# Second chunk of batch 0 in pairs of head pairs, and earlier exps in batches 2 and 3

## The chip, the cores and the metric

The kernel runs on one core of a Trainium2 chip. A core has five engines with instruction streams of their own: TensorE (matmul; weight loads are shown apart, as PEld), VectorE (DVE), ScalarE (ACT), GpSimd (POOL) and SyncE (SP), which here issues DMAs only. The metric is device time in microseconds for one whole execution. Before the change it is 401.13 us, the median of 3 runs (400.8 to 401.75).

## The reference, cut to what matters

Eight batches, eight heads, 1024 positions, head size 64. Keys and values are first projected along the sequence to 64 rows, then comes ordinary attention, then a feed-forward layer that takes the largest of three products.

```python
k_proj = np.einsum('ks,bhsd->bhkd', E, k)
v_proj = np.einsum('ks,bhsd->bhkd', F, v)
scores = scale * np.matmul(q, k_proj.transpose(0, 1, 3, 2))
attn = softmax(scores)
a = np.matmul(attn, v_proj)            # then heads are joined to x: 8192 x 512
h = np.maximum(np.maximum(x @ w1, x @ w2), x @ w3)   # 512 -> 768
out = h @ w_out                        # 768 -> 512
```

## The kernel before, in words

A batch is 1024 tokens, worked on in two chunks of 512 (`ch` 0 and 1). The attention works on head pairs: `g` counts the 4 pairs, `hp` the two heads in a pair. The feed-forward layer of a batch runs step by step, and the attention of the next batch is put between its steps.

**A chunk of the feed-forward layer.** `up` has six steps (`jt` 0 to 5), each with 12 matmuls of 128x512 (3 weight matrices by 4 blocks `ct`, line 600). ScalarE copies the first product out (`h1s`, line 665), VectorE takes the two maxima (lines 669 and 610; the last writes `hT`). Then `down` has four steps of 6 matmuls (line 708), each copied out to `o_sb` (by VectorE in batch 0, by ScalarE later) and stored by SP. The very first chunk of all has another order, `up_first`: it sweeps over w1, then over w2, then over w3, holding one bank for each of the six `jt`; a sweep does the first two `ct` for all `jt` ("a"), then the last two, with a max per `jt`.

**The order is written out.** `plan(b)` gives, by chunk and step, the functions that are issued behind that step. Steps 0 to 5 are those of `up`, 6 to 9 are `down`. [...] `then` in `up_first` does the same for the first chunk, with keys such as (2, 4): sweep 2 (w3), `jt` 4. Work put in `later` is issued at the next `run_later`, which comes behind the `h1s` copy of an `up` step or the o_sb copy of a `down` step.

**Banks.** Everything that TensorE writes goes to the eight banks of PSUM. `bank()` and `two()` (an even pair) choose the bank, or the pair, that is free first by the planner's own running clock (`clock`, `free`); this happens while the program is built. On the chip the choice only decides what a matmul has to wait for: the last reader of that bank.

**Attention of one head pair.** `scores` (line 221): four matmuls on quarters of the array (64*64) into two banks. `exps` (line 232): ScalarE's exp, to `pT`. Then either `za`, which has `sums` (ones times `pT`), `values` (`vp` times `pT`, both line 241), `invert` (ScalarE: ln to `zl`, line 301, and exp of its negative to `zi`, line 307) and `scale_x` (VectorE: product to `xT`, line 318); or, from batch 2 on, `zc`, which forms the sums of all four head pairs in one bank by eight matmuls (line 266), inverts them at once and spreads them through DRAM (`zd`, `zi_all`), with `vx` for values and scale. `sc(..., now=True)` issues the exp at once; without it, the exp goes to `later`.

**Batch 0.** Only its first chunk's attention is done before the feed-forward layer starts. The attention of its second chunk (`c1`: positions 4 to 7) is done one head pair at a time, between the w3 sweep and `down` of the first chunk; all its instructions have half the columns (256 per matmul, 512 per exp). It must be in `xT` before `up(0, 1, 0)`, whose first three matmuls per weight matrix read head pairs 0, 1 and 2; pair 3 is read at the end of the step.

**q of later batches.** `qd(b)` packs q by four VectorE copies to `q_p` (line 102) and has SP issue a DMA transpose to `qT` (line 421), for batch 1 in two halves. The next load of q, by POOL's queue, waits for the last of them.

Of the kernel before, what the change touches and what calls it, by code (L numbers as in the profile page):

```python
# [15 lines left out]
def kernel(  # L16
# [13 lines left out]
    nc = tc.nc  # L30
# [46 lines left out]
    def two():  # L77
        n = min(range(0, 8, 2), key=lambda n: max(free[n:n + 2]))
        deal((n, n + 1))
        return psum_t[:, n:n + 2, :], (n, n + 1)  # L80
# [6 lines left out]
    def pe(dt, wait=0.0):  # L87
        clock["pe"] = max(clock["pe"], wait) + dt
        return clock["pe"]

    def runs(eng, ready, dt, ns=()):
        if eng in clock:
            clock[eng] = max(clock[eng], ready + 0.06) + dt
            for n in ns:
                free[n] = clock[eng]
            return clock[eng]
        return ready + dt
# [3 lines left out]
    def copy(eng, o, i, ns=(), dt=0.65):  # L101
        done = {  # L102
            "v": nc.vector.tensor_copy, "s": nc.scalar.copy, "g": nc.gpsimd.tensor_copy
        }[eng](out=o, in_=i)
        runs(eng, clock["pe"] if ns else 0.0, dt, ns)
        return done
# [100 lines left out]
    def k_pair(b, g):  # L207
        if b in turned:
            return kpTs[b][:, g % 2, (g // 2) * KP:(g // 2 + 1) * KP]
        return kpTs[b][:, g, :]  # L210
# [3 lines left out]
    def scores(b, g, lo, nsi):  # L214
        t, ns = two()
        n = nsi // 2
        for c in range(2):
            for hp in range(2):
                rows = slice(hp * HALF, (hp + 1) * HALF)
                at = g * SI + lo + c * n  # L220
                nc.tensor.matmul(  # L221
                    out=t[c * HALF:(c + 1) * HALF, hp, 0:n * P],
                    lhsT=k_pair(b, g)[rows],
                    rhs=qTs[b][rows, at:at + n, :],
                    start=True, stop=True,
                )
        return t[:, :, 0:n * P], ns, pe(n * MM / 4 + 0.1)
# [20 lines left out]
    def sums(b, g, lo, nsi):  # L248
        return pair_mm(b, g, lo, nsi, lambda rows, hp: ones[rows])
# [48 lines left out]
    def invert(b, g, lo, nsi, z):  # L298
        t, ns, ready = z
        zl = att.tile([P, 2, CHUNK], FP32, name="zl", bufs=1)[:, :, 0:nsi * HALF]  # L300
        nc.scalar.activation(out=zl, in_=t, func=AF.Ln)  # L301
        runs("s", ready, 0.17 + nsi * 0.107, ns)
        if nsi == SI:
            zi = zi_all(b)[:, g]
        else:
            zi = att.tile([P, 2, CHUNK // 2], FP32, name="zi0", bufs=4)
        nc.scalar.activation(out=zi, in_=zl, func=AF.Exp, scale=-1.0)  # L307
        zis[b, g, lo] = zi, runs("s", ready, 0.17 + nsi * 0.107)

    def values(b, g, lo, nsi):  # L310
        if b not in xTs:
            xTs[b] = att.tile([P, NCT, SI, P], BF16, name="xT")
        return pair_mm(b, g, lo, nsi, lambda rows, hp: vps[b][rows, 2 * g + hp, :])
# [17 lines left out]
    def sc(b, g, lo=0, nsi=SI, now=False):  # L331
        def f():
            t = scores(b, g, lo, nsi)
            if now:
                exps(b, g, lo, nsi, t)
            else:
                later.append(lambda: exps(b, g, lo, nsi, t))
        return f

    def za(b, g, lo=0, nsi=SI, then=False):  # L340
        def f():
            z = sums(b, g, lo, nsi)
            av = values(b, g, lo, nsi)
            invert(b, g, lo, nsi, z)
            if then:
                later.append(lambda: scale_x(b, g, lo, nsi, av))
            else:
                scale_x(b, g, lo, nsi, av)
        return f
# [56 lines left out]
            )  # L406
        return f

    def qd(b, parts=1):

        def f():
            q_p = att.tile([P, NPAIR, SI, 2, D], BF16, name="q_p", bufs=1)
            qTs[b] = att.tile([P, NPAIR * SI, P], BF16, name="qT")
            n = NPAIR // parts
            for lo in range(0, NPAIR, n):
                for g in range(lo, lo + n):
                    copy(
                        "v", q_p[:, g].rearrange("p si h d -> p h si d"),
                        qkv[b][0][:, 2 * g:2 * g + 2], (), 0.43,
                    )  # L420
                last_T[b] = nc.sync.dma_start_transpose(
                    out=qTs[b][:, lo * SI:(lo + n) * SI, :],
                    in_=q_p[:, lo:lo + n].rearrange("p g si h d -> p (g si h d)"),
                )
        return f

    kps = {}
    def kproj(b):
# [312 lines left out]
    def plan(b):  # L741
        n = b + 1
        if b == 0:
            c1 = (SPC, SPC)
            return {
                (0, 6): [za(0, 1, *c1), sc(0, 3, *c1)],
                (0, 7): [qd(1, 2), store_now, za(0, 2, *c1)],
                (0, 8): [za(0, 3, *c1)],
                (1, 1): [kproj(1)],
                (1, 2): [kt(1)],  # L750
                (1, 3): [sc(1, 0, now=True), sc(1, 1), vproj(1), ld(2)],
                (1, 4): [za(1, 0), sc(1, 2, now=True)],
                (1, 5): [za(1, 1), sc(1, 3)],
                (1, 7): [za(1, 2)],
                (1, 8): [za(1, 3)],
            }
        if b == 1:
            return {
                (0, 0): [qd(2)],
                (0, 3): [kproj(2), vproj(2), ld(3, (0,))],  # L760
                (0, 4): [kt(2)],
                (0, 5): [sc(2, 0, now=True), sc(2, 1, now=True), sc(2, 2)],
                (0, 6): [sc(2, 3)],
                (0, 8): [zc(2, nc.gpsimd), ld(3, (1, 2))],
                (1, 1): [qd(3)],
                (1, 3): [vx(2, 0), vx(2, 1)],
                (1, 6): [vx(2, 2), vx(2, 3)],
            }
        if b == 2:
            return {  # L770
                (0, 2): [kproj(3), vproj(3), ld(4)],
                (0, 3): [kt(3)],
                (0, 4): [sc(3, 0, now=True), sc(3, 1)],
                (0, 5): [sc(3, 2, now=True), sc(3, 3)],
                (0, 7): [zc(3)],
                (0, 8): [qd(4)],
                (1, 3): [kproj(4), vproj(4), ld(5), vx(3, 0), vx(3, 1)],
                (1, 4): [kt(4)],
                (1, 7): [vx(3, 2), vx(3, 3), sc(4, 0)],
            }  # L780
        if n == B:
            return {}
        out = {
            (0, 1): [sc(n, 1, now=True), sc(n, 2, now=True), sc(n, 3)],
            (0, 3): [zc(n)],
            (1, 2): [vx(n, 0), vx(n, 1)],
            (1, 6): [vx(n, 2), vx(n, 3)],
        }
        if n + 1 < B:
            out[0, 4] = [qd(n + 1)]  # L790
            out[1, 2] = [kproj(n + 1), kd(n + 1), vproj(n + 1)] + out[1, 2]
            out[1, 6] += [sc(n + 1, 0)]
        if n + 2 < B:
            out[1, 3] = [ld(n + 2)]
        return out

    for b in range(B):
        p = plan(b)

        def behind(ch, step):  # L800
            for f in p.get((ch, step), []):
                f()

        for ch in range(NCHUNK):
            if (b, ch) == (0, 0):
                c1 = (SPC, SPC)
                up_first({
                    (0, 0, 1): [lambda: x(1)],
                    (0, 0, 3): [lambda: z(2), lambda: z(3)],
                    (0, 1, 1): [lambda: v_pair(2)],  # L810
                    (0, 1, 3): [lambda: x(2)],
                    (0, 1, 5): [lambda: v_pair(3), ld(1)],
                    (0, 2, 1): [lambda: x(3)],
                    (2, "a", 0): [pack_q(0, (0, 1), *c1)],
                    (2, "a", 1): [pack_q(0, (2, 3), *c1)],
                    (2, "a", 3): [qp(0, (0, 1), *c1)],
                    (2, "a", 5): [qp(0, (2, 3), *c1)],
                    (2, 1): [sc(0, 0, *c1)],
                    (2, 2): [sc(0, 1, *c1)],
                    (2, 4): [za(0, 0, *c1, then=True), sc(0, 2, *c1)],  # L820
                })
                run_later()
                behind(0, NJT - 1)
            else:
                for step in range(NJT):
                    up(b, ch, step, lambda: behind(ch, (step, "mid")))
                    behind(ch, step)
            for tt in range(SPC):
                down(b, ch, tt, "v" if b == 0 else "s")
                behind(ch, NJT + tt)  # L830
# [30 lines left out]
```

## Time and profile before

| | |
|---|---|
| Median of 3 runs | 401.13 us |
| The profiled execution's own time | 401.58 us |
| Its span, first to last instruction | 399.8 us |
| TensorE busy | 388.2 us, 97% of the span |
| VectorE busy | 203.0 us, 51% |
| ScalarE busy | 151.4 us, 38% |
| GpSimd busy | 34.4 us, 9% |
| Granted TensorE clock | full, 1.00 |

In a line of the profile stand the engine, the line of the kernel, the operation, what is written and read, the shape and the count. In a timeline a line starts with its start and its length in us; instructions of one kind that follow each other are merged, and `x4` tells how many. A bracket at the end names the idle time of the engine just before, and what ended it. Matmul ends are modelled, so lines may overlap a little, and some matmul records can be missing: a group of six can stand there with five. SPq is the queue of SP; its rows are the issuing of DMAs, not their transfer.

### The profile page before, as it was taken

How to read it: one execution, taken by the hardware profiler on the slowest of the kernel's cores; microseconds unless marked ns; L12 is line 12 of the kernel's file. 1: busy time of each engine (PE TensorE's matmuls, PEld its weight loads, DVE VectorE, ACT ScalarE, POOL GpSimd, SP SyncE). 2: the span in 40 equal slices, each digit the busy share in tenths (PEclk: the TensorE clock that was granted, in tenths of full speed). 3: DMA queues.
4: the chain of work that ended last, by engine and by line, in shares of the span. 5: the costliest groups of instructions: out<-in, count | busy, mean ns of one | idle time of the engine just before them, and what ended most of it. 6: DMA issues, size and time to landing. Idle time of an engine off the chain costs nothing.

```text
span 399.8 us, 5713 instructions
## 1 busy us (share of the span) xinstructions
PE 388.2 (97%) x2244; PEld 176.5 (44%) x2286; DVE 203.0 (51%) x316; ACT 151.4 (38%) x243; POOL 34.4 (9%) x49
## 2 busy tenths in 40 slices
PE   6899999999999999999999999999999999999996
PEld 3544443453444445444454445444454444444443
DVE  2348756761674525736273544744266342745251
ACT  2534538527222452263323532245323533132322
POOL 7350011000400200110002000200000000000000
PEclk9999999999999999999999999999999999999999
DMA  8999999977899998999989979696980229020203
GB/s 145 206 206 207 205 242 144 240 148 155 217 186 207 209 224 185 239 174 206 217 218 132 254 161 266 106 228 132 212 216 20 89 75 244 0 105 2 105 0 107
DMA packets 67340, 66.31 MB, mean 166 GB/s; under 512 B 31505, under 2 KB 59793, under 8 KB 67313
## 3 DMA queue, kind: packets, MB, share of 16 engines
q0 software_dynamic: 29104, 30.41, 47.3%
q1 hardware_dynamic: 38064, 35.46, 34.9%
q8 instruction: 18, 0.29, 0.3%
q10 hardware_dynamic: 144, 0.07, 0.1%
q14 instruction: 10, 0.07, 0.1%
HBM read 69.73 MB, written 16.97 MB: 217 GB/s over the span
## 4 chain that ended last, share of the span: by engine, by line
PE 87%; DMA 7%; POOL 2%; ACT 2%; issue 1%; DVE 1%; ACTq 0%; POOLq 0%
PE banks L600 59%; PE banks L708 19%; DMA qT<-q_p 4%; DMA v_t<-in_v_dram 3%; PE banks L355 3%; PE banks L241 2%; PE banks L221 2%; PE banks L266 1%; ACT zl L301 1%; ACT zi_all L307 1%; POOL k_t L152 0%; POOL q_t L157 0%; POOL v_t L152 0%; PE banks L688 0%; DVE xT L318 0%
## 5 line engine op out<-in xcount | busy, mean ns | idle before, releaser
L600 PE MATMUL banks<-xT,w_sb 128*128 128x512 bf16 x1119 | 254.7, 379 | 2.5 <-issue 0.6
L600 PEld LDWEIGHTS <-w_sb 128*128 128x128 bf16 x1152 | 110.1, 98 | 136.4 <-issue 8.1
L669 DVE TENSOR_TENSOR m<-banks,h1s 128x512 f32<-128x512 f32 x90 | 62.1, 690 | 134.7 <-ACT h1s L665 90.9
L665 ACT COPY h1s<-banks 128x512 f32<-128x512 f32 x90 | 52.6, 585 | 122.2 <-PE banks L600 120.7
L708 PE MATMUL banks<-wout_sb,hT 128*128 128x512 bf16 x370 | 85.8, 379 | 0.9 <-issue 0.6
L610 DVE TENSOR_TENSOR hT<-banks,m 128x512 bf16<-128x512 f32 x90 | 62.3, 692 | 9.4
L708 PEld LDWEIGHTS <-hT 128*128 128x128 bf16 x378 | 35.3, 98 | 47.4 <-issue 5.6
L102 ACT COPY o_sb<-banks 128x512 f32<-128x512 f32 (+2 forms) x57 | 32.8, 577 | 58.2 <-PE banks L708 57.9
L232 ACT ACTIVATE pT<-banks 128x1024 bf16<-128x1024 f32 (+1 forms) x36 | 32.8, 931 | 18.5 <-PE banks L221 18.5
L318 DVE TENSOR_TENSOR xT<-banks,zi_all 128x1024 bf16<-128x1024 f32 x28 | 33.1, 1220 | 11.7 <-PE banks L241 6.9
L201 POOL DMA_DIRECT2D q_t<-in_q_dram x7 | 6.1, 878 | 197.9 <-DMA qT<-q_p 118.1
L102 DVE CAST vp<-banks 64x256 bf16<-64x256 f32 (+1 forms) x18 | 7.1, 397 | 11.9 <-ACT vp L102 9.0
L355 PEld LDWEIGHTS <-efT 128*64 128x64 bf16 x224 | 11.6, 110 | 3.4 <-issue 3.4
L102 ACT CAST vp<-banks 64x256 bf16<-64x256 f32 x14 | 5.1, 364 | 18.4 <-PE banks L355 18.3
L221 PE MATMUL banks<-qT,kpT 64*64 64x512 bf16 (+1 forms) x144 | 11.4, 362 | 0.6 <-DVE m L669 0.3
L241 PE MATMUL banks<-pT,vp 64*64 64x512 bf16 (+1 forms) x144 | 11.4, 364 | 0.3 <-DVE vp L102 0.2
L301 ACT ACTIVATE zl<-banks 128x512 f32<-128x512 f32 (+1 forms) x12 | 8.9, 739 | 5.6 <-PE banks L241 4.6
L102 DVE COPY q_p<-q_t 128x1024 bf16<-128x1024 bf16 x28 | 10.5, 436 | 0.5 <-DMA q_t<-in_q_dram 0.5
L102 DVE COPY o_sb<-banks 128x512 f32<-128x512 f32 (+1 forms) x9 | 5.7, 639 | 4.5 <-PE banks L688 4.5
L355 PE MATMUL banks<-k_t,efT 128*64 128x256 bf16 x112 | 7.4, 276 | 0.0
L355 PE MATMUL banks<-v_t,efT 128*64 128x256 bf16 x112 | 7.3, 273 | 0.0
L478 PE MATMUL banks<-warm_f 128*128 128x512 f32 x8 | 5.8, 861 | 1.5 <-DVE warm_f L175 1.5
(63 smaller groups left out, 119.0 us busy)
## 6 DMA issues: line engine op xcount, KB each, us to landing
out_dram<-o_sb SPq DMA_DIRECT2D x30, 512.0 KB, 4.5
zi_all<-zd SPq DMA_DIRECT2D x20, 512.0 KB, 7.7
q_t<-in_q_dram POOLq DMA_DIRECT2D x7, 1024.0 KB, 10.4
k_t<-in_k_dram POOLq DMA_DIRECT2D x7, 1024.0 KB, 16.6
v_t<-in_v_dram POOLq DMA_DIRECT2D x7, 1024.0 KB, 21.5
zi_all<-zd POOLq DMA_DIRECT2D x4, 512.0 KB, 7.9
w_sb<-in_moe_w_dram POOLq DMA_DIRECT2D x4, 384.0 KB, 11.2
k_t<-in_k_dram POOLq DMA_DIRECT2D x2, 512.0 KB, 9.2
```

What stands on the lines that cost most here:

```text
L102: done = {"v": nc.vector.tensor_copy, "s": nc.scalar.copy, "g": nc.gpsimd.tensor_copy}[eng](out=o, in_=i)
L221: nc.tensor.matmul(out=t[c * HALF:(c + 1) * HALF, hp, 0:n * P], lhsT=k_pair(b, g)[rows], rhs=qTs[b][rows, at:at + n, :], start=True, stop= ...
L232: nc.scalar.activation(out=pTs[b, g, lo], in_=t, func=AF.Exp, scale=scale)
L241: nc.tensor.matmul(out=t[hp * HALF:(hp + 1) * HALF, c, 0:nsi * HALF], lhsT=w(rows, hp), rhs=p[rows, hp, :], start=True, stop=True,)
L301: nc.scalar.activation(out=zl, in_=t, func=AF.Ln)
L318: nc.vector.tensor_tensor(out=xTs[b][:, g, lo:lo + nsi, :].rearrange("a (c s) p -> a c (s p)", c=2), in0=t, in1=zi, op=ALU.mult,)
L355: nc.tensor.matmul(out=t[hh * HALF:(hh + 1) * HALF, 0:width], lhsT=efT[:, si, (kv - 1) * KP:kv * KP], rhs=qkv[b][kv][:, heads[hh], si, :], ...
L600: nc.tensor.matmul(out=h, lhsT=w_sb[i][:, ct, jt * P:(jt + 1) * P], rhs=xTs[b][:, ct, ch * SPC:(ch + 1) * SPC, :], start=(ct == first), st ...
L610: nc.vector.tensor_tensor(out=o, in0=h, in1=other, op=ALU.max)
L665: nc.scalar.copy(out=h1s, in_=h[0][0])
L669: nc.vector.tensor_tensor(out=m12, in0=h[1][0], in1=h1s, op=ALU.max)
L708: nc.tensor.matmul(out=o_ps, lhsT=hTs[b, ch][:, jt, tt * P:(tt + 1) * P], rhs=wout_sb[:, jt, :], start=(jt == 0), stop=(jt == NJT - 1),)
```

## The change

**Second chunk of batch 0.** Two head pairs go side by side in each bank. The new class `Duo` holds two head pairs (`u` 0: pairs 0 and 1, `u` 1: pairs 2 and 3); its methods issue eight matmuls of 256 columns where four were issued per head pair, and one exp, ln, exp or product of 1024 columns where two of 512 were. The attention is visited behind (2, 1) with the scores of duo 0, behind (2, 4) with its sums and values and the scores of duo 1, and behind the first `down` step, (0, 6), with the sums and values of duo 1. The visits behind (2, 2), (0, 7) and (0, 8) are gone from TensorE; VectorE's and ScalarE's parts are placed by hand.

**q of batch 1.** Behind (0, 7) the first two copies to `q_p` stay on VectorE, with their transpose; the scale of duo 1 follows; the other two copies go to ScalarE, with their transpose; `store_now`, the held-back store, comes last.

**Batches 2 and 3.** The exp of the fourth head pair is issued at once instead of at the next `run_later`.

```diff
-    def qd(b, parts=1):
+    def qd(b, gs=range(NPAIR), eng="v"):
...
+    class Duo:
+        def __init__(self, u, lo):
+            self.u, self.lo, self.n = u, lo, SPC * HALF
+        def part(self, t, gi):
+            return t[:, :, gi * self.n:(gi + 1) * self.n]
+        def scores(self):
+            t, ns = two()
+            for gi in range(2):
+                for c in range(2):
+                    for hp in range(2):
+                        rows = slice(hp * HALF, (hp + 1) * HALF)
+                        at = (2 * self.u + gi) * SI + self.lo + c * SPC // 2
+                        nc.tensor.matmul(
+                            out=self.part(t, gi)[c * HALF:(c + 1) * HALF, hp],
+                            lhsT=k_pair(0, 2 * self.u + gi)[rows],
+                            rhs=qTs[0][rows, at:at + SPC // 2, :],
+                            start=True, stop=True,
+                        )
+            ready = pe(0.3)
+            self.p = att.tile([P, 2, CHUNK], BF16, name="pT", bufs=6)
+            nc.scalar.activation(out=self.p, in_=t, func=AF.Exp, scale=scale)
+            runs("s", ready, 1.03, ns)
+        def pairs(self, w):
...
+        def sums(self):
+            t, ns, ready = self.pairs(lambda rows, h: ones[rows])
+            self.zl = att.tile([P, 2, CHUNK], FP32, name="zl", bufs=1)
+            nc.scalar.activation(out=self.zl, in_=t, func=AF.Ln)
+            runs("s", ready, 1.03, ns)
+        def values(self):
+            self.av = self.pairs(lambda rows, h: vps[0][rows, h, :])
+        def invert(self):
+            self.zi = zi_all(0)[:, self.u]
+            nc.scalar.activation(out=self.zi, in_=self.zl, func=AF.Exp, scale=-1.0)
+            self.when = runs("s", clock["pe"], 1.06)
+        def scale(self):
+            t, ns, ready = self.av
+            nc.vector.tensor_tensor(
+                out=xTs[0][:, 2 * self.u:2 * self.u + 2, self.lo:self.lo + SPC, :]
+                .rearrange("a g (c s) p -> a c g (s p)", c=2),
+                in0=t.rearrange("a c (g x) -> a c g x", g=2),
+                in1=self.zi.rearrange("a c (g x) -> a c g x", g=2), op=ALU.mult,
+            )
+            runs("v", max(ready, self.when), 1.22, ns)
...
-                (0, 6): [za(0, 1, *c1), sc(0, 3, *c1)],
-                (0, 7): [qd(1, 2), store_now, za(0, 2, *c1)],
-                (0, 8): [za(0, 3, *c1)],
+                (0, 6): [
+                    duo[1].sums, duo[1].values, duo[0].scale, duo[1].invert,
+                ],
+                (0, 7): [
+                    qd(1, range(2)), duo[1].scale, qd(1, range(2, 4), "s"), store_now,
+                ],
...
-                (0, 6): [sc(2, 3)],
+                (0, 6): [sc(2, 3, now=True)],
...
-                (0, 5): [sc(3, 2, now=True), sc(3, 3)],
+                (0, 5): [sc(3, 2, now=True), sc(3, 3, now=True)],
...
-                    (2, 1): [sc(0, 0, *c1)],
-                    (2, 2): [sc(0, 1, *c1)],
-                    (2, 4): [za(0, 0, *c1, then=True), sc(0, 2, *c1)],
+                    (2, 1): [duo[0].scores],
+                    (2, 4): [
+                        duo[0].sums, duo[0].values, duo[1].scores, duo[0].invert,
+                    ],
```

## The prediction

> **What bounds the kernel now.** I read the page's busy shares and chain first, then the timeline of TensorE through the stretch that the diff rewrites, then the matmuls of `zc`, then the chain around 150 to 170 us.
>
> ```profile
> PE 388.2 (97%) x2244; PEld 176.5 (44%) x2286; DVE 203.0 (51%) x316; ACT 151.4 (38%) x243; POOL 34.4 (9%) x49
> ...
> PE 87%; DMA 7%; POOL 2%; ACT 2%; issue 1%; DVE 1%; ACTq 0%; POOLq 0%
> ```
>
> TensorE is the bound: what makes its stream shorter, or takes a wait out of it, is gained, and nothing else counts unless TensorE is made to wait. The stream around the change (start, length, count):
>
> ```profile
> 35.26 0.81 PE L600 MATMUL banks<-xT,w_sb 128*128 128x512 bf16 x3
> 36.00 0.30 PE L221 MATMUL banks<-qT,kpT 64*64 64x256 bf16 x4
> 36.24 0.60 PE L600 MATMUL banks<-xT,w_sb 128*128 128x512 bf16 x2
> 37.01 0.30 PE L221 MATMUL banks<-qT,kpT 64*64 64x256 bf16 x4 [0.16 <-ACT pT L232]
> 37.24 1.04 PE L600 MATMUL banks<-xT,w_sb 128*128 128x512 bf16 x4
> ...
> 38.87 0.61 PE L600 MATMUL banks<-xT,w_sb 128*128 128x512 bf16 x2
> 39.31 1.46 PE L708 MATMUL banks<-wout_sb,hT 128*128 128x512 bf16 x6
> ...
> 41.38 1.24 PE L708 MATMUL banks<-wout_sb,hT 128*128 128x512 bf16 x5 [0.16 <-issue]
> ...
> 43.14 1.47 PE L708 MATMUL banks<-wout_sb,hT 128*128 128x512 bf16 x6
> 44.54 0.30 PE L241 MATMUL banks<-pT,ones 64*64 64x256 bf16 x4
> 44.67 0.28 PE L241 MATMUL banks<-pT,vp 64*64 64x256 bf16 x4
> 44.89 1.47 PE L708 MATMUL banks<-wout_sb,hT 128*128 128x512 bf16 x6
> 46.19 4.05 PE L600 MATMUL banks<-xT,w_sb 128*128 128x512 bf16 x17
> ```
>
> A 512-column matmul starts every 0.216 us (46.19 less 44.89, by six). What a visit to the attention takes is the distance between two long rows, less 0.216 per long matmul. The x5 row is a group of six with one record missing, so the visit before it is shorter by 0.216:
> - visit of (2, 1): 36.24-35.26-3x0.216 = 0.33, one group of four small matmuls
> - (2, 2): 37.24-36.24-2x0.216 = 0.57, one group; the row says that it waits for an exp, 0.24 over the first
> - (2, 4): 38.87-37.24-4x0.216 = 0.77, three groups
> - (0, 6): 41.38-39.31-6x0.216-0.216 = 0.56, three groups
> - (0, 7): 43.14-41.38-5x0.216 = 0.68, two groups
> - (0, 8): 44.89-43.14-6x0.216 = 0.45, two groups.
>
> Together 3.36. An undisturbed visit is 0.33 with one group, 0.45 with two and 0.56 with three: each further group costs 0.115, so going in and out costs 0.215. Against that (2, 4) waits 0.2 and (0, 7) 0.23; with (2, 2), 0.67 us of the six visits is waiting.
>
> **First part: the three visits of the duos.** All twelve groups remain, so clean visits would be 0.45 (two groups), 0.91 (six) and 0.68 (four), 2.04. At the switch a rule of the Trainium skill is weighed. The row: 0.215 per visit, so three visits fewer save 0.65. The rule: "TensorEngine Tiling (Array Packing)", section "Key Properties", says that a change of tiling mode drains the engine, and "TensorE: Matmul & The Clock Gate", section "Step-by-step: what each phase is for", puts a drain at about 128 cycles of 2.4 GHz, 0.053 us. One at each of two switches would be an estimate of 0.11 per visit, 0.32 for three. The row is twice that and is taken; by the rule the forecast would end 0.33 later.
>
> New waits, followed with the old durations. ACT rows are 0.60 for 512 columns and 1.03 (exp, `zl`) or 1.06 (`zi_all`) for 1024; a max on VectorE is 0.68 at a pitch of 0.60, a 1024-column `xT` scale 1.22. Banks come from the planner's own clock, gone through by hand from its state at (2, 1): `duo[0].scores` takes pair 2/3, its sums 6/7, its values 2/3, `duo[1].scores` 4/5, the first down bank 6, `duo[1].sums` 4/5, values 0/1.
> - 36.00 scores of duo 0 (eight matmuls); exp 36.47 to 37.50. Long matmuls from 36.36 on, six of them; the second visit starts 37.75, after that exp: the 0.24 wait of (2, 2) is gone.
> - 37.75 sums, values, and at 38.20 scores of duo 1. Bank 5 still belongs to the fourth max of the last w3 sweep (jt 3), which ends 38.33: a wait of 0.2, as (2, 4) has now. The visit ends 38.75.
> - `zl` of duo 0 runs 38.22 to 39.25 and holds bank 6, which the first down group wants at 39.18: a new wait of 0.13. Behind it on TensorE is everything.
> - exp of duo 1 ends 40.2; third visit 40.70 to 41.30, no wait. Three down groups, and the first `up` of chunk 1 starts at 45.18 instead of 46.19.
>
> So the first part gives 3.36-(2.04+0.2+0.13) = 1.0 us.
>
> What hides the rest. VectorE: o_sb 40.80, duo 0 scale 41.45 to 42.67 (its `zi` is ready at 41.3), o_sb, two q_p copies 43.42 to 44.16, duo 1 scale to 45.35. The third matmul of that `up` reads head pair 2 at 45.6: cover 0.25, and beyond it each us costs one. The new scale has a four-dimensional output pattern that no row shows; nearest is the 1.22 us scale of the same 1024 elements. Below nothing it can't help; if each took 0.5 longer, 0.75 would be lost. I take 1.22. ScalarE does two q_p copies of 1024 elements after `zi` of duo 1 (43.4). The second rule weighed: VectorE's four copies are one row,
>
> ```profile
> 43.61 1.42 DVE L102 COPY q_p<-q_t 128x1024 bf16<-128x1024 bf16 x4
> ```
>
> so some 0.35 apiece, while ScalarE's 512-element q_p copies take 0.61. "ScalarE: Activation LUTs", section "What ACT_TABLE_LOAD costs", gives one element per cycle for every type, 0.186 us + 0.833 ns each: 1.04 a copy, which speaks against the move; twice the row would be 1.22. The second half is ready at 45.5 or 45.9. Neither costs anything: SP is held by the first half until 51.3,
>
> ```profile
> 44.39 11.74 SPq L421 DMA_TRANSPOSE qT<-q_p  x2
> ```
>
> and its next ScalarE work, `h1s`, is due at 47.5. `store_now` sits behind both transposes on SP as before, and POOL's next load still waits for the second one. The first half's landing (44.39+12.1 by the DMA view, 56.5) doesn't move with TensorE, which now asks for it at 56.9 instead of 57.9: cover 0.4, and lost one for one beyond. In chunk 1 the bank choices come out as the same pattern with other numbers, so its waits (some 0.9 us from 65 to 76, for exps, a max and a scale) stay.
>
> **Second part: exps at once.** The exp of the fourth head pair now comes in front of an o_sb copy instead of behind the next one, and `zc` needs it:
>
> ```profile
> 96.24 1.03 ACT L232 ACTIVATE pT<-banks 128x1024 bf16<-128x1024 f32 x1
> 96.94 0.97 PE L266 MATMUL banks<-pT,pick 128*32 128x512 bf16 x8
> 97.84 1.47 PE L708 MATMUL banks<-wout_sb,hT 128*128 128x512 bf16 x6
> ```
>
> From the first `zc` matmul to the next long one is 0.90 here and in batch 3 (142.82 to 143.72). A later batch, whose exps are long done, shows 0.55:
>
> ```profile
> 182.47 0.62 PE L266 MATMUL banks<-pT,pick 128*32 128x512 bf16 x8
> 183.02 1.25 PE L600 MATMUL banks<-xT,w_sb 128*128 128x512 bf16 x5
> ```
>
> The exp moves from 96.24 to 95.5 (right behind the one before it) and from 142.12 to 141.05: done before 96.9 and 142.8. Gain 2x0.35 = 0.70. The o_sb copy queued behind waits up to 0.8; its bank isn't wanted soon and its store has slack.
>
> **Where some of it is given back.** One transfer has no slack:
>
> ```profile
> 153.59 14.56 DMA qT<-q_p
> ...
> 168.19 0.41 PE banks L221 x4
> ```
>
> Batch 4's scores wait for this landing, already 0.28 us. By then TensorE is 1.7 early. The landing's chain hangs on the program's progress (qT of batch 3 issued at 107.10, behind VectorE; its landing releases batch 4's loads; these crowd `zd` from 145.11 to 150.7, which releases `zi_all` and then this transpose), so it comes earlier by the 1.35 gained before 107; whether the last 0.35 gets through the crowd is open: cost 0 to 0.35, I take 0.2.
>
> **Sum.** 1.0+0.7-0.2 = 1.5: the profiled span 399.8 becomes 398.3, the profiled execution's own 401.58 becomes 400.1; it lies 0.45 over the median shown, 401.13, which becomes 399.6. About 0.2% (0.8 us) is what a measurement of this kernel can tell from no change.
>
> **Rivals.**
> - The first part comes to almost nothing: a bank falls otherwise than by my hand count, or the wide scale is slow, and TensorE waits in the duos as it did in the six visits. For it: three covers there are under 0.4 us. Against: ScalarE and VectorE lose fixed costs (1.2 becomes 1.03 per pair). Then only 0.7 is left: 400.4.
> - Nothing is gained, for the landing at 168.15 is set by the DMA engines' load and stays put: TensorE gives all of it back there, 401.1. For it: DMA shares at 1.2 from 107 to 150. Against: around 85 to 100 that share is 0.77, so the backlog starts anew behind program progress.
> - Slower: the qT transpose of batch 4 lands later than now. `zd` needed 5.6 us there against 2.4 at 230.83, because batch 4's loads fill the queues; `zi_all` and the transpose queue behind it on SP, and a meeting with other packets could cost some us. TensorE pays one for one: from a landing at 169.0 (0.8 later than now) the kernel is slower by over 0.2%; at 169.2, 402.2. Against: all its sources move earlier together.
>
> **How the numbers follow.** Forecast 0.66, centre 399.6, own range 399.0 to 400.2; little gained in the duos 0.13; nothing gained 0.10; slower 0.11. The range leaves out under 2 in 10 if it reaches from 399.0 to the no-gain case at 401.2. Faster by over 0.8: the forecast and half of the first rival, 0.71; within 0.2%: the other half and the no-gain case, 0.17; slower 0.12.
>
> **What would show it.** Three visits between 36 and 41.5; the first `up` of chunk 1 at 45.2; a 0.2 wait for a max in the second visit and 0.13 before the first down group; `zc` at 0.55 in batches 2 and 3; scores of batch 4 near 166.6 with a wait of 0.3 to 0.6 for the transpose. It would be wrong if that `up` starts after 46, if TensorE waits for the xT scale at 45.6 or for qT at 56.9, or if batch 4's scores start at 168 or later.

## The result, and the profile after

The changed kernel takes 399.44 us (median of 6 runs, 398.88 to 399.63), the kernel before 400.97 in the same comparison (6 runs): 0.9961 of it, 95% interval 0.9947 to 0.9974. That is 1.53 us faster, and by the interval between 1.0 and 2.1; 1.5 was forecast. (Ratios, here and below, are worked out from all the runs, and needn't equal the quotient of the two medians.) The profiled execution took 399.43 us with a span of 397.7; the one of before had 401.58 and 399.8.

Line numbers have moved: the matmuls of `up` are now line 668, those of `down` line 776, the maxima lines 678 and 737, and `Duo` has lines 446 (scores), 454 (exp), 463 (sums and values), 474 and 482 (ln, inverse) and 487 (scale). The timeline of TensorE in the changed kernel, through the stretch that was rewritten:

```profile
35.72 0.41 PE L446 MATMUL banks<-qT,kpT 64*64 64x256 bf16 x8
36.06 1.47 PE L668 MATMUL banks<-xT,w_sb 128*128 128x512 bf16 x6
37.47 0.41 PE L463 MATMUL banks<-pT,ones 64*64 64x256 bf16 x8
37.71 0.39 PE L463 MATMUL banks<-pT,vp 64*64 64x256 bf16 x8
37.92 0.58 PE L446 MATMUL banks<-qT,kpT 64*64 64x256 bf16 x8
38.44 0.60 PE L668 MATMUL banks<-xT,w_sb 128*128 128x512 bf16 x2
39.05 1.46 PE L776 MATMUL banks<-wout_sb,hT 128*128 128x512 bf16 x6
40.44 0.41 PE L463 MATMUL banks<-pT,ones 64*64 64x256 bf16 x8
40.68 0.39 PE L463 MATMUL banks<-pT,vp 64*64 64x256 bf16 x8
41.00 4.06 PE L776 MATMUL banks<-wout_sb,hT 128*128 128x512 bf16 x18
44.90 3.40 PE L668 MATMUL banks<-xT,w_sb 128*128 128x512 bf16 x15
```

From the first visit to the first `up` of chunk 1 it is 44.90-35.72 = 9.18 us, where before it was 46.19-36.00 = 10.19. The six long matmuls between the first two visits have no visit among them any more. Two small waits are in these rows: the scores row of 0.58 is 0.17 longer than the first, and from the second `up` matmul at 38.66 (38.44 and 0.216) to `down` at 39.05 it is 0.39 where 0.216 would do.

The first sum matmul and the long row behind it, in `zc` of batch 2 and of batch 3:

```profile
95.66 0.62 PE L266 MATMUL banks<-pT,pick 128*32 128x512 bf16 x8
96.20 1.47 PE L776 MATMUL banks<-wout_sb,hT 128*128 128x512 bf16 x6
...
141.19 0.61 PE L266 MATMUL banks<-pT,pick 128*32 128x512 bf16 x8
141.74 2.76 PE L776 MATMUL banks<-wout_sb,hT 128*128 128x512 bf16 x12
```

0.54 and 0.55 us, where it was 0.90 each time: 0.71 less. Batch 3's rows before the change, for comparison, and then ScalarE's exps in batch 2 after it, the last two of the four in one row:

```profile
142.82 0.97 PE L266 MATMUL banks<-pT,pick 128*32 128x512 bf16 x8
143.72 2.55 PE L708 MATMUL banks<-wout_sb,hT 128*128 128x512 bf16 x11
...
93.21 1.96 ACT L232 ACTIVATE pT<-banks 128x1024 bf16<-128x1024 f32 x2
```

The last exp ends at 95.17, half a microsecond before `zc` begins at 95.66; before the change it ran from 96.24 to 97.27, and `zc` had begun at 96.94. The values of batch 3's last head pair and the scores of batch 4 behind them, before and after:

```profile
167.44 0.63 PE L241 MATMUL banks<-pT,vp 64*64 64x512 bf16 x8
168.19 0.41 PE L221 MATMUL banks<-qT,kpT 64*64 64x512 bf16 x4
...
165.45 0.63 PE L241 MATMUL banks<-pT,vp 64*64 64x512 bf16 x8
166.05 0.41 PE L221 MATMUL banks<-qT,kpT 64*64 64x512 bf16 x4
```

0.60 from one row to the other; it was 0.75, and it is 0.45 where TensorE doesn't have to wait for the transpose (166.42 less 165.96 in the run with all q copies first is 0.46). So the wait for the transpose shrank from 0.30 to 0.15. From those scores to the end it is the same: 231.6 us in both. The spans differ by 2.1, which the rows make up to a rounding: 1.01 in the rewritten stretch, 0.71 in `zc`, 0.15 at the transpose, and 0.28 that isn't the change's, for the first visit itself came at 35.72 instead of 36.00. That is a difference between two executions: the wait for a load of v at 20.6 us, 0.25 in the execution of before, is missing in this one. The medians, less bound to single starts, say 1.5.

### The profile page after: what moved, and what is told of

Read it like the earlier page. It is cut to its first block, busy times and chain, and to the rows that moved or that the text cites. A ratio compares the mean times of both kernels' runs of the same rounds, so it can differ in the third digit from the quotient of the medians.

```text
span 397.7 us, 5745 instructions
## 1 busy us (share of the span) xinstructions
PE 390.7 (98%) x2286; PEld 176.7 (44%) x2286; DVE 201.9 (51%) x312; ACT 152.3 (38%) x239; POOL 34.5 (9%) x49
## 4 chain that ended last, share of the span: by engine, by line
PE 93%; DVE 2%; DMA 2%; ACT 1%; issue 1%; POOL 0%; DVEq 0%; ACTq 0%; POOLq 0%
PE banks L668 61%; PE banks L776 20%; PE banks L355 3%; PE banks L241 2%; DMA k_t<-in_k_dram 2%; PE banks L221 2%; DVE xT L318 1%; PE banks L266 1%; ACT zi_all L307 1%; ACT zl L301 1%; PE banks L575 1%; DVE m L737 0%; PE banks L546 0%; PE banks L601 0%; PE banks L756 0%
## 5 line engine op out<-in xcount | busy, mean ns | idle before, releaser
L318 DVE TENSOR_TENSOR xT<-banks,zi_all 128x1024 bf16<-128x1024 f32 x28 | 33.1, 1220 | 11.7 <-PE banks L241 6.9
L232 ACT ACTIVATE pT<-banks 128x1024 bf16<-128x1024 f32 (+1 forms) x32 | 30.2, 974 | 15.4 <-PE banks L221 15.4
L102 DVE CAST vp<-banks 64x256 bf16<-64x256 f32 (+1 forms) x18 | 7.1, 397 | 11.7 <-ACT vp L102 9.0
L241 PE MATMUL banks<-pT,vp 64*64 64x512 bf16 (+1 forms) x128 | 10.3, 375 | 0.2 <-DVE vp L102 0.2
L221 PE MATMUL banks<-qT,kpT 64*64 64x512 bf16 (+1 forms) x128 | 9.7, 372 | 0.4 <-DVE m L737 0.4
L102 DVE COPY q_p<-q_t 128x1024 bf16<-128x1024 bf16 x26 | 9.7, 433 | 0.5 <-DMA q_t<-in_q_dram 0.5
L546 PE MATMUL banks<-warm_f 128*128 128x512 f32 x8 | 6.6, 977 | 1.5 <-DVE warm_f L175 1.5
L301 ACT ACTIVATE zl<-banks 128x512 f32<-128x512 f32 (+1 forms) x8 | 6.5, 811 | 3.3 <-PE banks L241 3.1
```

What stands on the lines that cost most here:

```text
L102: done = {"v": nc.vector.tensor_copy, "s": nc.scalar.copy, "g": nc.gpsimd.tensor_copy}[eng](out=o, in_=i)
L221: nc.tensor.matmul(out=t[c * HALF:(c + 1) * HALF, hp, 0:n * P], lhsT=k_pair(b, g)[rows], rhs=qTs[b][rows, at:at + n, :], start=True, stop= ...
L232: nc.scalar.activation(out=pTs[b, g, lo], in_=t, func=AF.Exp, scale=scale)
L241: nc.tensor.matmul(out=t[hp * HALF:(hp + 1) * HALF, c, 0:nsi * HALF], lhsT=w(rows, hp), rhs=p[rows, hp, :], start=True, stop=True,)
L318: nc.vector.tensor_tensor(out=xTs[b][:, g, lo:lo + nsi, :].rearrange("a (c s) p -> a c (s p)", c=2), in0=t, in1=zi, op=ALU.mult,)
```

## The experiments

**The duos alone.** The changed kernel with the two exps put back:

```diff
-                (0, 6): [sc(2, 3, now=True)],
+                (0, 6): [sc(2, 3)],
...
-                (0, 5): [sc(3, 2, now=True), sc(3, 3, now=True)],
+                (0, 5): [sc(3, 2, now=True), sc(3, 3)],
```

> The duos and the q copies alone; the two exps of batches 2 and 3 are back behind the o_sb copy. Theory: the rewritten stretch gives 1.0 us, the two zc visits stay at 0.90 us each from the first sum matmul to the next long one, batch 4's transpose moves with the program, so the time is 1.0 below the kernel before (0.9975 of it) and TensorE's wait for that transpose stays near 0.28 us. Rival, that the transpose is held by the load on the DMA engines: it lands at 168 as before, TensorE waits 1.3 us for it, and the time is as before.

Measured: 399.98 us against 400.85, 0.9983 of the kernel before (0.9974 to 0.9991); the 0.9975 expected lies near the edge of that. The stretch is 9.18 us as in the changed kernel, `zc` has its old length, and batch 4's scores come at 166.68:

```profile
95.62 0.97 PE L266 MATMUL banks<-pT,pick 128*32 128x512 bf16 x8
96.52 1.47 PE L776 MATMUL banks<-wout_sb,hT 128*128 128x512 bf16 x6
...
166.12 0.63 PE L241 MATMUL banks<-pT,vp 64*64 64x512 bf16 x8
166.68 0.41 PE L221 MATMUL banks<-qT,kpT 64*64 64x512 bf16 x4
```

The last distance is 0.56, so TensorE waits 0.1 there, and not the 0.28 expected, though it comes 1.3 us earlier (0.3 of that from an earlier start). The transpose landed before 166.7 and not at 168: the rival that the load on the DMA engines keeps it at 168 is out.

**The exps alone.** The kernel before with the same two lines changed the other way:

```diff
-                (0, 6): [sc(2, 3)],
+                (0, 6): [sc(2, 3, now=True)],
...
-                (0, 5): [sc(3, 2, now=True), sc(3, 3)],
+                (0, 5): [sc(3, 2, now=True), sc(3, 3, now=True)],
```

> The kernel before with only the two exps issued at once. Theory: both zc visits go from 0.90 to 0.55 us, 0.70 in all, and batch 4's transpose lands 0.5 to 0.9 earlier than before, so 0.5 to 0.8 us below the kernel before (0.998 to 0.9987). Rival: zc's first visit gains, but the wait for the transpose of batch 4 grows by 0.35 or 0.7, and the time is 0.35 below or the same.

Measured: 400.26 against 400.85, 0.9988 (0.998 to 0.9997), at the edge of what was expected. The rewritten stretch keeps its 10.19 us, and the first rows of `zc` and those at batch 4 are

```profile
96.15 0.62 PE L266 MATMUL banks<-pT,pick 128*32 128x512 bf16 x8
96.70 1.47 PE L708 MATMUL banks<-wout_sb,hT 128*128 128x512 bf16 x6
...
165.95 0.63 PE L241 MATMUL banks<-pT,vp 64*64 64x512 bf16 x8
166.41 0.41 PE L221 MATMUL banks<-qT,kpT 64*64 64x512 bf16 x4
```

0.55, and 0.46 without a wait. The two parts together (0.9983 times 0.9988 is 0.9971) lie within the interval of the whole, so the times don't contradict that the parts add up; the rows, which are the same in the parts as in the whole, show it better.

**A visit more.** Does a change into the small mode (quarters of the array, 64*64) and back cost what the six visits seemed to say? In batches 4 to 7, far from anything else, one head pair's scores get a visit of their own:

```diff
-            (0, 1): [sc(n, 1, now=True), sc(n, 2, now=True), sc(n, 3)],
+            (0, 1): [sc(n, 1, now=True), sc(n, 2, now=True)],
+            (0, 2): [sc(n, 3, now=True)],
```

> The changed kernel with the scores of the fourth head pair of batches 4 to 7 taken out of the visit behind (0, 1) and given a visit of their own behind (0, 2), exp at once: four changes into the 64*64 mode and back more, and no other matmul more. Price of a visit as the rows of the six visits had it, 0.215 us: 0.86 us over the changed kernel from 170 us on. One drain of 128 cycles at each end, as worked out from the page: 0.43 us. Nothing, if the change of mode is hidden: under 0.1 us.

Measured: 400.01 us against 400.85 (0.9981, 0.9972 to 0.999), and from batch 4's scores to the end 232.52 us instead of 231.61. First the changed kernel, then this one, in batch 3's first chunk:

```profile
174.27 0.84 PE L221 MATMUL banks<-qT,kpT 64*64 64x512 bf16 x12
175.04 5.35 PE L668 MATMUL banks<-xT,w_sb 128*128 128x512 bf16 x24
180.33 0.61 PE L266 MATMUL banks<-pT,pick 128*32 128x512 bf16 x8
```

```profile
174.61 0.63 PE L221 MATMUL banks<-qT,kpT 64*64 64x512 bf16 x8
175.17 2.76 PE L668 MATMUL banks<-xT,w_sb 128*128 128x512 bf16 x12
177.87 0.41 PE L221 MATMUL banks<-qT,kpT 64*64 64x512 bf16 x4
178.21 2.76 PE L668 MATMUL banks<-xT,w_sb 128*128 128x512 bf16 x12
180.90 0.61 PE L266 MATMUL banks<-pT,pick 128*32 128x512 bf16 x8
...
165.20 0.63 PE L241 MATMUL banks<-pT,vp 64*64 64x512 bf16 x8
166.40 0.41 PE L221 MATMUL banks<-qT,kpT 64*64 64x512 bf16 x4 [0.57 <-DMA qT<-q_p]
```

From the first scores row to the `zc` row it is 6.06 us, and 6.29 with the visit more: 0.23 for the same 36 matmuls; four times that is 0.92, and 0.91 was found. The price taken from the rows is about right, and the 0.11 worked out from one drain at each switch is half of it. The last two rows show something else: up to there this program is the changed kernel's, yet here the wait for the transpose is 1.20-0.45 = 0.75.

**All q copies ahead of the scale.** Is the move of two copies to ScalarE needed?

```diff
-                    qd(1, range(2)), duo[1].scale, qd(1, range(2, 4), "s"), store_now,
+                    qd(1, range(2)), qd(1, range(2, 4)), duo[1].scale, store_now,
```

> The changed kernel with all four q copies of batch 1 on VectorE ahead of duo 1's scale, instead of two on ScalarE behind it. The scale ends 0.7 us later; the cover over it in the changed kernel is 0.27 us (its end at 45.00, third matmul of that up at 45.33, 0.06 for the release). Theory: TensorE waits 0.4 to 0.5 us at the third matmul of the first up of chunk 1, and the kernel is that much slower than the changed one. Rival, the cover is larger or something else ends later: no wait there.

Measured: VectorE's row of the scale, and TensorE's two rows around the wait:

```profile
44.57 1.22 DVE L487 TENSOR_TENSOR xT<-banks,zi_all 128x1024 bf16<-128x1024 f32 x1
...
45.02 0.59 PE L668 MATMUL banks<-xT,w_sb 128*128 128x512 bf16 x2
45.84 1.46 PE L668 MATMUL banks<-xT,w_sb 128*128 128x512 bf16 x6 [0.23 <-DVE xT L487]
```

The scale, issued behind all four copies, ends 9.95 us after the first visit, where it was 9.28 in the changed kernel. Two matmuls run, and the third starts 0.05 after the end of the scale (45.79), 0.39 later than its turn at 45.45. So it is that scale which is late next, and having two copies on ScalarE is what keeps it off the path. The whole time, 399.60 against 400.85 (0.9972, 0.9959 to 0.9985), doesn't tell 0.4 from the changed kernel; the row does.

**Another bank for the first down group.** The planner is told that the two banks of `zl` are free 1 us later than it thinks:

```diff
             runs("s", ready, 1.03, ns)
+            for n in ns:
+                free[n] += 1.0
```

> The changed kernel with the planner's clock for the two banks of zl put 1 us later, so that the first down group takes the bank of the fifth max instead of a bank that zl still holds. Theory: the 0.17 us that TensorE waits there (0.386 from start to start instead of 0.216) go, and from the first visit to the first up of chunk 1 it is 9.01 us instead of 9.18. Rival, the last hT, which that group's sixth matmul reads, is the next thing late: 0.1 or less is gained.

Measured, in one execution (399.70 us): first visit at 36.23, first `up` of chunk 1 at 45.25, 9.02 us. The group follows without a wait, 0.44 for two matmuls:

```profile
38.96 0.60 PE L670 MATMUL banks<-xT,w_sb 128*128 128x512 bf16 x2
39.40 1.46 PE L778 MATMUL banks<-wout_sb,hT 128*128 128x512 bf16 x6
```

So the wait was the bank's, worth 0.16. That is too little for one whole time to show.

**Looking for more in chunk 1 of batch 0.** There TensorE waits 0.63 us for a max before batch 1's last scores (65.55), and 0.32 for a scale (74.7). First the scores alone are moved behind the first down step, then the sums and values too, then that with the other bank:

```diff
-                (1, 5): [za(1, 1), sc(1, 3)],
-                (1, 7): [za(1, 2)],
-                (1, 8): [za(1, 3)],
+                (1, 5): [za(1, 1)],
+                (1, 6): [sc(1, 3, now=True), za(1, 2)],
+                (1, 7): [za(1, 3)],
```

(That is the second; the first has only `sc(1, 3, now=True)` in (1, 6) and leaves the `za` where they were.)

> The changed kernel with the scores of batch 1's fourth head pair moved from behind step (1, 5) of batch 0, where they wait 0.63 us for the max of that step (0.848 from start to start, 0.22 without a wait), to a visit of their own behind (1, 6), exp at once. Theory: the wait of 0.63 goes and a visit more costs the 0.23 measured, so 0.4 us are gained up to the first up of batch 1. Rival, the wait moves to another instruction behind the same late scale on VectorE: nothing gained, or 0.2 lost.

> As the run before, and za of the third and fourth head pairs of batch 1 one down step earlier, behind (1, 6) and (1, 7): as many visits as in the changed kernel. Theory: the 0.63 us goes without a visit more, and the ln, exp and scale that the first up of batch 1 waits for (0.33 us at 74.7) end about 1 us earlier, so that wait goes too: 0.9 us below the changed kernel, 2.4 below the kernel before (0.994). Rival, VectorE is blocked behind the scale that waits for its zi, so that the o_sb copies free their banks late and TensorE waits for a bank in the down steps: 0.6 or less.

> The run before together with the other bank for the first down group: 0.1 to 0.17 us less than it, 1.0 to 1.1 below the changed kernel, if the two are independent (0.9935 of the kernel before).

Measured: 399.42 us (0.9959, 0.9943 to 0.9974), 399.80 (0.9976, 0.9961 to 0.9991) and 399.57 (0.996, 0.9946 to 0.9973), all against 400.81: none can be told from the changed kernel's 0.9961 on the good side, and 0.994 and 0.9935 had been expected of the last two. In the first, the 0.63 is gone, but 0.23 goes to the new visit and 0.22 to a wait for the last `hT` inside the down group, which now starts earlier, so 0.18 is left of the 0.4 expected. In the second, TensorE's rows behind the first down group are

```profile
66.89 0.41 PE L221 MATMUL banks<-qT,kpT 64*64 64x512 bf16 x4
67.13 0.39 PE L241 MATMUL banks<-pT,ones 64*64 64x512 bf16 x4
68.43 0.41 PE L241 MATMUL banks<-pT,vp 64*64 64x512 bf16 x4 [0.91 <-ACT pT L232]
```

The values wait for a bank that the exp holds, some 1.07 us by the distance to the sums (1.30 against 0.23); that exp itself starts only at 67.35, behind the inverse of the head pair before. The wait at 74.7 is gone as expected, and more than the two waits (0.95) is lost here, 1.07 for the bank and 0.2 for the last `hT` as in the first: I had named VectorE's copies as what could hold the banks, and it was ScalarE's exp. With the other bank, it is 0.12 shorter from the first visit to batch 2's key projection (47.71 against 47.83 us), so the two edits add up, but not to a gain: the changed kernel takes 47.46.

The first of these also met the other transpose. Its timeline at batch 1's first scores:

```profile
55.73 0.59 PE L668 MATMUL banks<-xT,w_sb 128*128 128x512 bf16 x2
56.75 0.63 PE L221 MATMUL banks<-qT,kpT 64*64 64x512 bf16 x8 [0.43 <-DMA qT<-q_p]
```

1.02 us for two long matmuls and a switch, where 0.53 is usual (0.216, and some 0.31 from the start of the last long matmul to the first small one): 0.5 lost, in a stretch whose program is the changed kernel's.

## Why the prediction was right

- **The rewritten stretch, 1.0 us.** It was 1.01. Visits, waits and banks came where the working had put them, 0.28 earlier for the start: second visit 37.47 (forecast 37.75), `down` 39.05 (39.31), third visit 40.44 (40.70), `up` 44.90 (45.18). The wait of 0.13 before `down` was 0.17, and the other bank took it away. The wait of 0.2 in the second visit was 0.17; no run moved its bank, so that it is the fourth max's is the working's word alone.
- **0.215 for a switch.** It was 0.23 in four visits added on purpose. With the drain as the Trainium skill has it ("TensorE: Matmul & The Clock Gate", "Step-by-step: what each phase is for"), this stretch would have been forecast 0.33 too long.
- **Cover of 0.25 over the wide scale.** The scale took the 1.22 us assumed for its four-dimensional pattern, ended 45.00, and its reader came at 45.33: 0.27 with the release. Putting two copies more in front of the scale cost 0.39.
- **The q copies on ScalarE.** They took 1.97 us for two, 43.0 to 45.0 (forecast 43.4 to 45.5 by the rule, 45.9 by twice the 512-element row). That is 0.99 apiece, near the 1.04 of the Trainium skill ("ScalarE: Activation LUTs", "What ACT_TABLE_LOAD costs") and far from 1.22. SP's second transpose was not delayed by it, for the first held SP until 50.8.
- **0.70 in `zc`.** It was 0.71, and alone it gave 0.9988.
- **The giveback of 0.2 at batch 4's transpose.** This term was wrong, in sign too: the wait became shorter by 0.15. I took it that the landing would move less than TensorE does. SP's rows, before and after, show that the transpose was issued 2.39 earlier, where TensorE came 1.99 earlier (167.44 to 165.45):

```profile
145.11 0.50 SPq L278 DMA_DIRECT2D zd<-zic  x1
153.59 12.56 SPq L421 DMA_TRANSPOSE qT<-q_p  x1
...
143.14 0.49 SPq L278 DMA_DIRECT2D zd<-zic  x1
151.20 12.83 SPq L424 DMA_TRANSPOSE qT<-q_p  x1
```

`zd`, the transfer at the head of that chain, moved by 1.97 like TensorE and then landed in 5.2 us instead of 5.6, which is the other 0.4; the transpose itself took 14.8 from issue to landing, 14.6 before. Neither length is fixed by the program: in the run with a visit more, whose program is the changed kernel's up to there, `zd` took 5.6 and the transpose 15.0, and the wait was 0.75. Over the ten profiles `zd` took 5.2 to 5.8, the transpose 14.3 to 15.0, and the wait was 0.30 before, 0.15 after, 0.1 with the duos alone, 0.25 in the last two of the runs above and under 0.05 in the other four. It doesn't follow how early TensorE comes: 0.25 in the second of the last three runs, where the values before it start at 166.05, none in the first of them at 165.47, 0.15 in the changed kernel at 165.45.

That 1.5 met 1.53 this closely is therefore luck: without this term the forecast would have been 1.7, and the measured interval, 1.0 to 2.1, holds both.

- **The cover of 0.4 at batch 1's first transpose.** It was 0.4 to 0.5 in the profile after (issue at 43.90 and 12.2 to the landing, TensorE's turn at 56.56), and in one of the runs above it was used up and 0.5 more. Before the change it was 1.4: TensorE asked at 57.86 for what landed at about 56.5. The change has made a wait possible there that was not, and the step that named it took the landing as fixed. How often it strikes the changed kernel is open; its own profile shows no wait. Whether the other bank shows in the whole time is open too, for it was timed in one execution only.
- **The chances.** The forecast and half of the first rival make 0.66 and 0.065, so the chance of more than 0.8 us was 0.73 by its own terms, not 0.71.

## What to carry to other kernels

Where TensorE is the bound and short bursts in another tiling mode lie between its long matmuls, read the price of a burst as the distance between the long rows less the long matmuls in it: it splits into the switch, the work and the wait, and the three call for different edits. An exp that is put off behind a copy costs something only where its reader comes soon: 0.35 us here with 3 us from the scores to `zc` (93.91 to 96.94), nothing with 6 (174.27 to 180.33). To find such a place, look for the matmul row that is longer than its later copies. And once a stretch is shorter, go on to the transfers whose landing doesn't move with it, and count how much cover each has left, over more than one execution.

## What was not expected of the hardware

The landing of a transfer that shares the DMA engines with big loads differed by some tenths of a microsecond from one execution to the next, with the same program up to there: the first transpose of batch 1 took 12.2 us from issue to landing in the changed kernel's profile, 11.7 in the run with the sums moved too, and 13.0 in the run where TensorE waited for it. (The loads' queue alone had a share of 1.14 of the engines' time there, from 43 to 50 us.) Meanwhile TensorE's own stretches repeat: 9.17 or 9.18 us in every run that has the same program there, and 231.6 from batch 4's scores to the end in all but the one that adds visits. So a stretch of the trace shows 0.2 us which a median of whole times can't.
